# Selective attention and an MLP mixer in one kernel: loads issued behind transposing transfers, and a running sum behind transposes

## The chip, the cores and the metric

The kernel runs on one core of a Trainium2 chip. The time is the device time of one launch in microseconds (us). Several launches are timed and the median is given; one more is profiled.

The engines are called by the profile's names: PE is TensorE (matmuls, and transposes done as matmuls), ACT is ScalarE, DVE is VectorE, POOL is GpSimd, SP is SyncE. Loads of inputs are issued from POOL, outputs and transposing transfers from SP.

## The reference

There are 8 batches of 576 positions, 8 heads of width 64. Attention has an extra bias that comes from the running sum of `s`, and is followed by an MLP mixer over positions and then channels.

```python
scores = scale * np.matmul(q, k.transpose(0, 1, 3, 2))
cum = np.cumsum(np.maximum(s, 0.0), axis=-1)
bias = -(cum[:, :, :, None] - cum[:, :, None, :])
scores = np.where(causal, -1000000000.0, scores + np.minimum(bias, 0.0))
attn = softmax(scores)                  # over the last axis
x = concat_heads(np.matmul(attn, v))    # (8, 576, 512)
xt = x.transpose(0, 2, 1)
h = np.maximum(xt @ w_tok1, 0.0) @ w_tok2
u = x + h.transpose(0, 2, 1)
h2 = np.maximum(u @ w_ch1, 0.0) @ w_ch2
return u + h2
```

## The kernel before, in words

Batches have indices 0 to 7 here. For each of them the kernel records these steps:

- `stage_qk` and `stage_v` issue the loads from POOL: q and k of four heads at a time into a tile `qkn` (a ring of five), v in five parts into `vf` (two). `merge_v` multiplies v by the exponential of the running sum, giving `vp` (one tile for even indices, one for odd). `squares` reads `qkn` on ACT and sums its squares into `sq`, which a test at the end needs; for indices 0 and 1 it has loads of its own, in `stage_sq`.
- `quad` turns q and k of four heads on PE (L689, the 64x64 matmuls). `pair` makes the scores of two heads (L731), exponentials on ACT (L739), a causal mask on DVE (L748), the product with `vp` on PE (L802) and the normalisation on DVE.
- `tok` is the mixer over positions (L899, L961). It leaves u, and u turned, in a tile `uT` (`uTa` for even indices, `uTb` for odd). From index 2 on u is turned by transposing transfers that SP issues (L977), four for an even index and five for an odd one; the fifth reads `us`, the last 64 positions of two batches in one tile.
- `chan` is the mixer over channels: L1017 makes the hidden layer from `uT`, ACT or DVE applies the ReLU, L1042 makes the second layer, DVE adds u (L1050), and SP stores the result (L1055, L1058).

None of this is issued in the order of the record. `Plan.run` is a list scheduler in the kernel's own Python: each step has an engine (or a choice of two), an estimated duration, a priority, and dependencies from the tiles that it reads and writes. The scheduler keeps a clock for each engine and one for the DMA (`dma_free`, first free at 6.0), and adds margins to what waits for a DMA or for PE once its clock passes `STEADY`. The resulting start times give the order of each engine's instructions. On the chip the engines then run in that order and wait on semaphores. Steps with `after` keep a fixed order among themselves: `chain` holds all loads of POOL in the order of their record, and a load waits for the landing of the eighth before it.

The loads are recorded first, all of them: indices 0 and 1 with the weights between, then indices 2 to 7, then the second loads of indices 0 and 1 for their squares. After that come `quad`, `tok` and `chan` of each index. What holds a load back is thus the ring of its tile and the place in `chain`. Where the plan has PE idle in the first 45 us, matmuls on zeros fill it (L1135).

At the start the running sum is made on DVE: `s` is loaded, its ReLU taken (L532), the scan run (L534), half of its last value taken (L537); ACT makes the exponentials `wn` (L540), PE turns them (L560).

Of the kernel before, what the change touches and what calls it, by code (L numbers as in the profile page):

```python
# [8 lines left out]
FP32 = mybir.dt.float32  # L9
# [2 lines left out]
ALU = mybir.AluOpType  # L12


SWITCH = 0.095
STEADY = 50.0
MARGIN = 0.5
# [37 lines left out]
class Plan:  # L55
# [11 lines left out]
    def op(self, alts, reads=(), writes=(), prio=0, dma=0.0, holds=(), after=None, mode=0, lock=False, alone=None):  # L67
        o = Op()
        o.alts = alts
        o.prio = prio  # L70
        o.dma = dma
        o.mode = mode
        o.lock = lock
        o.alone = alone
        o.idx = len(self.ops)
        o.deps = set()
        o.users = []
        o.bufs = []
        for k in list(reads) + list(writes) + list(holds):
            b = k[0] if isinstance(k, tuple) else k  # L80
            if isinstance(b, Buf) and b not in o.bufs:
                o.bufs.append(b)
                b.left += 1
        for k in reads:
            w = self.writer.get(k)
            if w is not None:
                o.deps.add(w)
        for k in writes:
            w = self.writer.get(k)
            if w is not None:  # L90
# [12 lines left out]
        self.ops.append(o)  # L103
        return o

    def run(self, eps=0.03):
# [11 lines left out]
        for o in ops:  # L118
            if o.nd == 0:
                for e in o.alts:  # L120
                    cands[e].append(o)
        dma_free = 6.0
        mode = 0
        order = []

# [17 lines left out]
        while left:  # L143
            best = None
            for e in engines:
                lst = []
                tmin = None
                for o in cands[e]:
                    st = slot_time(o)
# [62 lines left out]
            for u in o.users:  # L212
                if u.after is o:
                    rdy = est + occ
                elif u.alts.keys() == {"PE"} and e == "PE":
                    rdy = est + occ
                elif e in u.alts and len(u.alts) == 1 and not o.dma:
                    rdy = est + occ
                else:
                    rdy = fin  # L220
                    if fin > STEADY:
                        rdy += MARGIN_DMA if o.dma else MARGIN if u.alts.keys() == {"PE"} else 0.0
                u.ready = max(u.ready, rdy)
# [144 lines left out]
def kernel(  # L368
# [18 lines left out]
    NJ = 5  # L387
# [15 lines left out]
    def sb(name, shape, dt, pool=None):  # L403
        return (pool or const).tile(shape, dt, name=name, tag=name)
# [44 lines left out]
    chain = []  # L449
    sent = []  # L450

    def load_op(fn, key, us, occ=0.75, prio=-1):

        o = P.op({"POOL": (occ, 0, fn)}, writes=key, prio=prio, dma=us, after=chain[-1] if chain else None)
        if len(sent) >= 8:
            o.deps.add(sent[-8])
        sent.append(o)
        chain.append(o)

    def load_cast(n, b, h, i, src):  # L460
        def load():
            nc.gpsimd.dma_start(  # L462
                out=n.t[:, i, :, :],
                in_=src[b, h : h + 4, :, :].rearrange("(f e) (p r) d -> (e p) f (r d)", e=2, r=R))
        load_op(load, [(n, i)], 1.45, prio=-1 if b or h else -3)

    qkn = {}

# [47 lines left out]
    for ti, src in enumerate((k, q)):  # L516
# [4 lines left out]
        for f in range(2):  # L521
# [9 lines left out]
         writes=["s"], prio=-7)  # L531
    P.op(dve(576, lambda: nc.vector.tensor_scalar_max(out=s_sb[:, :], in0=s_sb[:, :], scalar1=0.0)),  # L532
         reads=["s"], writes=["sr"], prio=-1)
    P.op({"DVE": (1.3, 1.6, lambda: nc.vector.tensor_tensor_scan(  # L534
        out=cum[:, :], data0=one_sb[:, :], data1=s_sb[:, :], initial=0.0, op0=ALU.mult, op1=ALU.add))},
        reads=["sr"], writes=["cum"], prio=-1)
    P.op(dve(1, lambda: nc.vector.tensor_scalar(  # L537
        out=half[:, :], in0=cum[:, S - 1 : S], scalar1=-0.5, scalar2=None, op0=ALU.mult)),
        reads=["cum"], writes=["half"], prio=-1)
# [59 lines left out]
    def stage_v(b, cs=tuple(range(NJ))):  # L599
        if b not in vbuf:  # L600
            vbuf[b] = Buf(r_vf), Buf(r_vp[b % 2])
        vf, vp = vbuf[b]
        odd = b % 2
        for c in cs:
            n = min(128, S - c * 128)
            p0 = 64 if odd and n < 128 else 0

            def load_first(c=c, n=n, p0=p0):
                nc.sync.dma_start(out=vf.t[p0 : p0 + n, c, :, :],
                                  in_=v[b, :, c * 128 : c * 128 + n, :].rearrange("h p d -> p h d"))  # L610

            def load(c=c, n=n, p0=p0):
                nc.gpsimd.dma_start(out=vf.t[p0 : p0 + n, c, :, :],  # L613
                                  in_=v[b, :, c * 128 : c * 128 + n, :].rearrange("h p d -> p h d"))
            if b == 0 and c == NJ - 1:
                P.op({"SP": (0.6, 5.5, load_first)}, writes=[(vf, c)], prio=-2)
                continue
            load_op(load, [(vf, c)], 1.15 * n / 128, 0.92)
        if b:
            merge_v(b, cs)  # L620

# [50 lines left out]
    def quad(b, h):  # L672
# [4 lines left out]
        for ti in range(2):  # L677
# [6 lines left out]
            def tr(ti=ti, pv=pv):  # L684
                for r in range(R):
                    for e in range(2):
                        p0 = e * PR
                        for f in range(2):
                            nc.tensor.transpose(out=pv(e)[f * D : f * D + D, r * PR : (r + 1) * PR],  # L689
                                                in_=nat.t[p0 : p0 + PR, ti, f, r * D : (r + 1) * D],  # L690
                                                identity=ident[p0 : p0 + PR, p0 : p0 + PR])
            P.op({"PE": (R * 0.031, R * 0.031 + 0.21, tr)}, reads=([(nat, ti, 0), (nat, ti, 1)] if b == 0 and h == 0 else [(nat, ti)]) + ["ident"] + pads,
                 writes=[(pts[e], e) for e in range(2)], holds=[d[ti] for d in dsts], prio=(np_ - 30 * (b < 1 and h < 1), 2), mode=1)
            for e in range(2):
                def ev(eng, ti=ti, e=e, pv=pv):
                    i = pv(e)[:, 0:S].rearrange("d (r p) -> d p r", r=R)
                    o = dsts[e][ti].t[:, 0:S].rearrange("d (p r) -> d p r", r=R)
                    if eng == 0:
                        nc.scalar.copy(out=o, in_=i)  # L699
                    else:  # L700
                        nc.vector.tensor_copy(out=o, in_=i)
                P.op({"ACT": (*c_act(576), lambda ev=ev: ev(0)), "DVE": (*c_dve(576), lambda ev=ev: ev(1))},
                     reads=[(pts[e], e)], writes=[(dsts[e][ti], 0)], prio=1, alone=pts[e])
# [378 lines left out]
    for i in range(2, 4):  # L1082
        load_ch2(i)
    stage_v(1)
    for b in range(2, B):
        stage_qk(b, 0)
        stage_v(b)
        stage_qk(b, 4)
    for b in range(2):
        for h in range(0, H, 4):  # L1090
            stage_sq(b, h)
    for b in range(B):
        for h in range(0, H, 4):
            quad(b, h)
        st = tok(b)
        chan(b, *st)

    P.op({"DVE": (1.3, 1.6, lambda: nc.vector.tensor_tensor_scan(
        out=pre[:, :], data0=one_sb[:, :], data1=wn[:, 0:S], initial=0.0, op0=ALU.mult, op1=ALU.add))},
# [84 lines left out]
```

## Time and profile before

| | before |
|---|---|
| median of three runs | 305.8 us (305.24 to 306.14) |
| the profiled execution | 306.06 us |
| its span, first to last instruction | 304.3 us |
| mean granted PE clock | 0.995 |
| PE busy | 291.8 us (96%) |
| ACT busy | 182.8 us (60%) |
| DVE busy | 172.0 us (57%) |
| POOL busy | 107.6 us (35%) |

Times in the profile count from the first instruction of the span. A row of a timeline gives start, length, engine, line and operation of a run of instructions of one kind, and in brackets the idle time of the engine before it and what ended that. A row of the chain of waits gives start, length, and what the time went to, along the path that ended last. A PE that is called busy is not at its peak, since matmuls are pipelined and their ends are modelled. POOL counts the making of a DMA's descriptors as busy.

### The profile page before, as it was taken

What the parts mean: (1) busy time and instruction counts of PE and PEld (TensorE: products, weight loads), DVE (VectorE), ACT (ScalarE), POOL (GpSimd) and SP (SyncE); (2) the same over time, 40 slices, a digit from 0 to 9 for tenths busy, and PEclk for the clock granted to TensorE, in tenths of its full rate; (3) what the DMA queues carried; (4) which work ended last, traced back from release to release, by engine and by line L of the source; (5) the groups of instructions that cost most, each with busy time, mean ns of one, the idle gap of its engine ahead of it and who ended that gap; (6) DMA issues with size and microseconds to landing.
All of it is one profiled execution on the core that took longest, in us unless ns stands there. A gap on an engine that the chain in (4) does not pass through costs nothing.

```text
span 304.3 us, 8094 instructions
## 1 busy us (share of the span) xinstructions
PE 291.8 (96%) x3430; PEld 168.2 (55%) x3430; DVE 172.0 (57%) x368; ACT 182.8 (60%) x298; POOL 107.6 (35%) x147
## 2 busy tenths in 40 slices
PE   8899999899999999999999999998999999999991
PEld 3478566467754545457754545455764544457550
DVE  5962889377976456756556556956456642420030
ACT  5887884699996486609872387727761286017300
POOL 8675469999780418107620108500000000000000
PEclk9999999999999999999999999999999999999998
DMA  8999999999997673358455535894004310250032
GB/s 218 226 207 206 216 224 229 252 190 262 227 156 125 155 197 54 79 140 178 94 80 103 133 84 83 132 116 136 2 2 84 125 38 0 69 155 2 0 111 74
DMA packets 38348, 39.29 MB, mean 129 GB/s; under 512 B 17600, under 2 KB 30976, under 8 KB 38304
## 3 DMA queue, kind: packets, MB, share of 16 engines
q0 software_dynamic: 17072, 24.25, 44.6%
q1 hardware_dynamic: 21232, 14.44, 18.7%
q8 instruction: 29, 0.48, 0.7%
q14 instruction: 15, 0.12, 0.1%
HBM read 40.65 MB, written 9.44 MB: 165 GB/s over the span
## 4 chain that ended last, share of the span: by engine, by line
PE 84%; DMA 12%; POOL 1%; issue 1%; DVE 0%; POOLq 0%
PE pmx L1017 30%; PE pmx L1042 30%; PE pmx L961 5%; PE pmx L899 5%; PE psc L802 5%; PE psc L731 5%; DMA qkn<-in_k_dram 5%; PE psc L689 3%; DMA wc<-in_moe_w_ch_dram 3%; DMA vf<-in_v_dram 2%; DMA uTb<-us 2%; POOL qkn L462 1%; PE pmx L986 0%; DVE of L1050 0%; POOL keep masks.py:66 0%
## 5 line engine op out<-in xcount | busy, mean ns | idle before, releaser
L1017 PEld LDWEIGHTS <-wc 128*128 128x128 bf16 x624 | 57.9, 98 | 32.6 <-issue 1.5
L739 ACT ACTIVATE E<-psc 128x1024 bf16<-128x1024 f32 x64 | 62.2, 1024 | 22.8 <-PE psc L731 22.2
L1017 PE MATMUL pmx<-uTb,wc 128*128 128x320 bf16 (+2 forms) x384 | 56.1, 299 | 1.4 <-DMA uTb<-ub 1.1
L1042 PE MATMUL pmx<-wc,gb 128*128 128x512 bf16 (+1 forms) x252 | 55.3, 369 | 0.0
L1017 PE MATMUL pmx<-uTa,wc 128*128 128x512 bf16 (+1 forms) x240 | 45.6, 337 | 0.0
L647 ACT ACTIVATE junk<-qkn 128x1152 bf16<-128x1152 bf16 x32 | 37.3, 1166 | 11.7 <-DMA qkn<-in_q_dram 11.3
L1042 PE MATMUL pmx<-wc,ga 128*128 128x512 bf16 x192 | 44.1, 379 | 0.0
L631 POOL TENSOR_TENSOR vp<-vf,wT 128x512 bf16<-128x512 f32 (+1 forms) x31 | 32.3, 1058 | 25.6 <-PE psc L802 24.9
L1024 ACT ACTIVATE gb<-pmx 128x320 bf16<-128x320 f32 (+2 forms) x57 | 24.7, 438 | 21.2 <-PE pmx L1017 17.3
L1042 PEld LDWEIGHTS <-gb 128*128 128x128 bf16 x252 | 23.6, 98 | 24.8 <-issue 0.2
L613 POOL DMA_DIRECT2D vf<-in_v_dram x39 | 34.1, 884 | 7.3 <-DMA qkn<-in_k_dram 2.2
L748 DVE TENSOR_TENSOR E<-E,keep 128x512 bf16<-128x512 bf16 x56 | 25.8, 474 | 13.3 <-ACT E L739 13.1
L1042 PEld LDWEIGHTS <-ga 128*128 128x128 bf16 x192 | 18.2, 98 | 20.4
L1024 ACT ACTIVATE ga<-pmx 128x512 bf16<-128x512 f32 (+1 forms) x36 | 19.2, 535 | 11.7 <-PE pmx L1017 11.1
L462 POOL DMA_DIRECT2D qkn<-in_k_dram x19 | 14.1, 744 | 33.5 <-issue 31.8
L1026 DVE TENSOR_SCALAR gb<-pmx 128x320 bf16<-128x320 f32 (+2 forms) x39 | 18.8, 487 | 11.9 <-PE pmx L1017 11.5
L699 ACT COPY kT<-psc 128x576 bf16<-128x576 bf16 x22 | 13.1, 641 | 19.4 <-PE psc L689 17.9
L802 PEld LDWEIGHTS <-E 128*128 128x128 bf16 x576 | 21.1, 97 | 5.5
L835 DVE TENSOR_TENSOR x<-psc,rc 128x640 bf16<-128x640 f32 x28 | 23.0, 823 | 0.9
L1050 DVE TENSOR_TENSOR of<-pmx,ua 128x512 f32<-128x512 f32 x16 | 11.0, 689 | 19.5 <-PE pmx L1042 19.3
L731 PE MATMUL psc<-qT,kT 64*128 64x256 bf16 (+2 forms) x320 | 21.3, 250 | 0.0
L731 PEld LDWEIGHTS <-kT 64*128 64x128 bf16 x320 | 12.6, 94 | 14.6 <-issue 11.5
(107 smaller groups left out, 300.9 us busy)
## 6 DMA issues: line engine op xcount, KB each, us to landing
vf<-in_v_dram POOLq DMA_DIRECT2D x32, 256.0 KB, 7.9
out_dram<-of SPq DMA_DIRECT2D x31, 256.0 KB, 2.3
qkn<-in_k_dram POOLq DMA_DIRECT2D x19, 288.0 KB, 6.7
qkn<-in_q_dram POOLq DMA_DIRECT2D x19, 288.0 KB, 7.3
wc<-in_moe_w_ch_dram POOLq DMA_DIRECT2D x8, 384.0 KB, 11.4
out_dram<-of SPq DMA_DIRECT2D x10, 128.0 KB, 2.3
vf<-in_v_dram POOLq DMA_DIRECT2D x7, 128.0 KB, 7.4
gb<-in_k_dram SPq DMA_DIRECT2D x1, 576.0 KB, 3.9
```

The lines of the kernel that those rows point to most:

```text
L613: nc.gpsimd.dma_start(out=vf.t[p0 : p0 + n, c, :, :], in_=v[b, :, c * 128 : c * 128 + n, :].rearrange("h p d -> p h d"))
L631: eng.tensor_tensor(out=vp.t[p0 : p0 + n, c, :, 0:D], in0=vf.t[p0 : p0 + n, c, :, :], in1=wT[p0 : p0 + n, cw, b * H : b * H + H].unsqueeze ...
L647: nc.scalar.activation(out=junk[:, :].rearrange("p (t n) -> p t n", t=2), in_=i, func=AF.Square, accum_out=sq[:, col : col + 1])
L731: nc.tensor.matmul(out=ps.t[:, hh * 512 + c0 : hh * 512 + c0 + e - a], lhsT=kT.t[hh * 64 : hh * 64 + 64, j0 : j0 + 128], rhs=qT.t[hh * 64 ...
L739: nc.scalar.activation(out=E.t[:, :, 512 * pc : 512 * pc + 512], in_=ps.t[:, :].rearrange("p (e n) -> p e n", e=2), func=AF.Exp, scale=0.125)
L748: nc.vector.tensor_tensor(out=o, in0=o, in1=keep[:, :].unsqueeze(1).unsqueeze(1).to_broadcast([128, 2, 2, 128]), op=ALU.mult)
L802: nc.tensor.matmul(out=o[:, ic, 0:DE], lhsT=E.t[:, hh, d0 : d0 + 128], rhs=vp.t[:, jc, h + 2 * hh, 0:DE], start=(jc == j_lo), stop=(jc == ic))
L835: nc.vector.tensor_tensor(out=x.t[:, :, :].rearrange("p c (g f e d) -> p g e f c d", f=2, e=2, d=D)[:, h // 4, h % 2], in0=pav2()[:, :, :, ...
L1017: nc.tensor.matmul(out=pm.t[:, 0 : e - a], lhsT=wc1[:, m, cc * 128 : cc * 128 + 128], rhs=uT.t[:, m, a:e], start=(m == 0), stop=(m == NMC ...
L1024: lambda cc=cc, pm=pm, a=a, e=e: nc.scalar.activation(out=g.t[:, cc, a:e], in_=pm.t[:, 0 : e - a], func=AF.Relu),
L1026: lambda cc=cc, pm=pm, a=a, e=e: nc.vector.tensor_scalar_max(out=g.t[:, cc, a:e], in0=pm.t[:, 0 : e - a], scalar1=0.0)),
L1042: nc.tensor.matmul(out=pm.t[:, na:ne], lhsT=g.t[:, cc, c * 128 : c * 128 + 128], rhs=wc2[:, cc, na:ne], start=(cc == 0), stop=(cc == NCC - 1))
```

## The change

- The loads of indices 4 to 7 are no longer recorded with the others at the front. They are recorded after `chan` of indices 2 to 5 (`stage_in(b + 2)`), behind a row of `touch` steps: copies of one element on POOL, each of which reads one chunk of `uT` of index `b` and so waits for the transposing transfer that wrote it. The touches stand in `chain`, and the loads behind them.
- The second loads of indices 0 and 1 are recorded behind the loads of indices 5 and 6.
- The scan of `s` waits, in the plan, for the transposes of q of the first four heads, and its priority among DVE's steps falls from -1 to 2.
- The plan's DMA is first free at 6.85 and not at 6.0. A touch is marked `bare`: the plan adds no margin to what it waits for.
- `probe`, `PACE0`, `PACE1` and `DEPTH` are prepared for touches between loads; with both `PACE` at 0 they issue nothing.

```diff
+DEPTH = 4
+PACE0, PACE1 = 0, 0
 ...
-        dma_free = 6.0
+        dma_free = 6.85
 ...
-                    if fin > STEADY:
+                    if fin > STEADY and not u.bare:
                         rdy += MARGIN_DMA if o.dma else MARGIN if u.alts.keys() == {"PE"} else 0.0
 ...
-    def load_op(fn, key, us, occ=0.75, prio=-1):
+    probes = []
+    seen = sb("seen", [128, 8], FP32, fast)
+
+    def touch(ap, reads, col):
+        o = P.op({"POOL": (0.12, 0.2, lambda: nc.gpsimd.tensor_copy(out=seen[0 : ap().shape[0], col : col + 1], in_=ap()))},
+             reads=reads, writes=[("seen", col)], prio=-1, after=chain[-1])
+        o.bare = True
+        chain.append(o)
+
+    def load_op(fn, key, us, occ=0.75, prio=-1, probe=None):
+        if PACE0 <= len(probes) < PACE1 and probes[-DEPTH]:
+            touch(probes[-DEPTH][0], probes[-DEPTH][1], 0)
+        probes.append((probe, key) if probe else None)
 ...
-    P.op({"DVE": (1.3, 1.6, lambda: nc.vector.tensor_tensor_scan(
+    scan = P.op({"DVE": (1.3, 1.6, lambda: nc.vector.tensor_tensor_scan(
         out=cum[:, :], data0=one_sb[:, :], data1=s_sb[:, :], initial=0.0, op0=ALU.mult, op1=ALU.add))},
-        reads=["sr"], writes=["cum"], prio=-1)
+        reads=["sr"], writes=["cum"], prio=2)
 ...
+            if b == 0 and h == 0 and ti == 1:
+                scan.deps.add(turn)
 ...
-    for b in range(2, B):
+    def stage_in(b):
         stage_qk(b, 0)
         stage_v(b)
         stage_qk(b, 4)
-    for b in range(2):
-        for h in range(0, H, 4):
-            stage_sq(b, h)
+    for b in range(2, 4):
+        stage_in(b)
     for b in range(B):
         for h in range(0, H, 4):
             quad(b, h)
         st = tok(b)
         chan(b, *st)
+        if 2 <= b < B - 2:
+            for c in range(NJ - 1 + b % 2):
+                touch(lambda c=c, uT=st[2]: uT.t[0:1, 0, c * 128 : c * 128 + 1], [(st[2], c)], 1)
+            stage_in(b + 2)
+            if b == 3 or b == 4:
+                for h in range(0, H, 4):
+                    stage_sq(b - 3, h)
```

More of the change, by code (lines that the diff above doesn't have):

```diff
@@ L77, in op @@
         o.users = []
+        o.bare = False
         o.bufs = []
@@ L464, in load @@
                 in_=src[b, h : h + 4, :, :].rearrange("(f e) (p r) d -> (e p) f (r d)", e=2, r=R))
-        load_op(load, [(n, i)], 1.45, prio=-1 if b or h else -3)
+        load_op(load, [(n, i)], 1.45, prio=-1 if b or h else -3, probe=lambda: n.t[0:1, i, 0, 0:1])
     qkn = {}
@@ L617, in stage_v @@
                 continue
-            load_op(load, [(vf, c)], 1.15 * n / 128, 0.92)
+            load_op(load, [(vf, c)], 1.15 * n / 128, 0.92, probe=lambda c=c, p0=p0: vf.t[p0 : p0 + 1, c, 0, 0:1])
         if b:
@@ L691, in tr @@
                                                 identity=ident[p0 : p0 + PR, p0 : p0 + PR])
-            P.op({"PE": (R * 0.031, R * 0.031 + 0.21, tr)}, reads=([(nat, ti, 0), (nat, ti, 1)] if b == 0 and h == 0 else [(nat, ti)]) + ["ident"] + pads,
+            turn = P.op({"PE": (R * 0.031, R * 0.031 + 0.21, tr)}, reads=([(nat, ti, 0), (nat, ti, 1)] if b == 0 and h == 0 else [(nat, ti)]) + ["ident"] + pads,
                  writes=[(pts[e], e) for e in range(2)], holds=[d[ti] for d in dsts], prio=(np_ - 30 * (b < 1 and h < 1), 2), mode=1)
+            if b == 0 and h == 0 and ti == 1:
+                scan.deps.add(turn)
             for e in range(2):
```

## The prediction

> **What bounds the kernel now.** I read the busy time by stretches first, because one share for the whole span hides where TensorE is not the limit. The columns behind each stretch are its length and then the busy time of PE, its weight loads, VectorE (DVE), ScalarE (ACT) and GpSimd (POOL).
>
> ```profile
> 20.00:36.00 16.00, 15.23 (x248) 11.37 (x246) 7.65 (x21) 12.69 (x27) 7.68 (x12) 1.00 1.21 207
> 54.00:60.00 6.00, 4.72 (x47) 2.56 (x46) 1.98 (x4) 3.36 (x5) 5.98 (x7) 1.00 1.05 243
> 60.00:200.00 140.00, 140.00 (x1666) 78.57 (x1663) 92.24 (x184) 97.64 (x152) 64.17 (x80) 1.00 0.70 137
> 200.00:208.00 8.00, 6.61 (x115) 3.53 (x112) 3.76 (x6) 2.50 (x5) 0.00 (x0) 1.00 1.40 175
> 208.00:297.60 89.60, 89.60 (x769) 50.72 (x766) 35.15 (x72) 39.64 (x70) 0.00 (x0) 1.00 0.20 56
> ```
>
> From 60 to 200 and from 208 to 297.6 us PE has no idle time at all, at a granted clock of 1.00. No edit of transfers can shorten those stretches; it can only lengthen them. What can be won lies in the holes: 0.77 us in 20:36, 1.28 in 54:60, 1.39 in 200:208. The timeline of PE names them (start, length, what, and in brackets the idle time before it and who ended it):
>
> ```profile
> 9.22 0.48 PE L689 MATMUL pmx<-ident,qkn 64*64 64x64 bf16 x36 [0.81 <-DMA qkn<-in_k_dram]
> ...
> 35.50 0.48 PE L689 MATMUL psc<-ident,qkn 64*64 64x64 bf16 x36 [0.62 <-DMA qkn<-in_k_dram]
> ...
> 56.08 0.38 PE L899 MATMUL pmx<-x,w 128*128 128x128 bf16 x4 [1.28 <-issue]
> ...
> 206.54 0.70 PE L1017 MATMUL pmx<-uTb,wc 128*128 128x320 bf16 x4 [1.06 <-DMA uTb<-ub]
> 207.57 1.26 PE L1017 MATMUL pmx<-uTb,wc 128*128 128x320 bf16 x8 [0.33 <-DMA uTb<-us]
> ```
>
> Two holes are loads of k that land late at the start, one (56.08) is ended by no engine and no transfer that the profile shows, and the last two, 1.06 + 0.33 = 1.39 us, are PE waiting for the transposing transfers of batch index 5 (the sixth batch).
>
> **The transfers of index 5: minus 1.4 us.** What is normal for them and what happened there is in the view of the tile uTb, first for the stretch 194:208, then for index 7 in 262:272:
>
> ```profile
> DMA to landing us min/median/max: 6.6/8.7/10.5
> ```
>
> ```profile
> DMA to landing us min/median/max: 2.4/2.5/2.5
> ```
>
> The difference is the company. GpSimd's timeline has the last two loads of the kernel (the second look at q and k of index 1, for the squares) issued in the middle of it; the three rows above them are a normal pair of k and q and the five parts of v, which I need below:
>
> ```profile
> 137.21 0.77 POOL L462 DMA_DIRECT2D qkn<-in_k_dram  x1 [14.18 <-issue]
> 137.98 0.72 POOL L462 DMA_DIRECT2D qkn<-in_q_dram  x1
> 138.69 4.25 POOL L613 DMA_DIRECT2D vf<-in_v_dram  x5
> ...
> 193.86 0.77 POOL L462 DMA_DIRECT2D qkn<-in_k_dram  x1 [0.92 <-ACT junk L647]
> 194.62 0.72 POOL L462 DMA_DIRECT2D qkn<-in_q_dram  x1
> ```
>
> After the change these second looks are issued with the loads of indices 5 and 6, behind the transfers of indices 3 and 4, and the loads of index 7 wait until the transfers of index 5 have landed. Nothing of GpSimd's queue is then in flight beside index 5, so its transfers should land in about 2.5 us and the 1.39 us go. Next in line on PE is the channel matmul itself, in order, with no other wait before it. I take all of it: -1.4 (bounds 0 if something else slows them, and -1.4; PE cannot give back more than it idles).
>
> **The start: minus 0.6 and minus 0.4.** Two edits act here. The planner's first free moment of the DMA moves from 6.0 to 6.85, so it expects each load later, and the running sum of s waits for the transposes of q. In the built order PE then places the scores of the first pair ahead of the transposes that idled 0.81 us at 9.22, and two more groups of channel matmuls of index 0 ahead of the transposes that idled 0.62 us at 35.50. The loads themselves stand in GpSimd's queue as before, so that load still lands at 35.5, but PE has less left to do by then. The hole at 35.50 is worth -0.6 (bounds -0.6 and 0). Of the hole at 9.22 I take half, -0.4: the first exponential comes earlier, but the weights exp(sum of s), and with them the scaled v, come later, and which of the two ends last I cannot read (bounds -0.8 and +0.4, the second as much lost as I expect won).
>
> **What the change adds.** Eighteen one-element copies on GpSimd (four or five for each of indices 2 to 5), each waiting for one transposing transfer. They are no longer than a DMA issue there, 0.77 us, so at most 14 us on an engine that is idle for 75.8 of the 140 us quoted above. What counts is what stands behind them in GpSimd's order: q, k and v of the batch two ahead, and the products of v (vp). The tight case is index 5, behind the transfers of index 3. SyncE's timeline gives when those are issued, and the tile views of qkn and vf in 137:143 give the landing of loads:
>
> ```profile
> 126.95 6.03 SPq L977 DMA_TRANSPOSE uTb<-ub  x4
> 133.08 1.21 SPq L977 DMA_TRANSPOSE uTb<-us  x1
> ...
> 262.96 5.12 SPq L977 DMA_TRANSPOSE uTb<-ub  x4
> 268.18 1.22 SPq L977 DMA_TRANSPOSE uTb<-us  x1
> ```
>
> ```profile
> DMA to landing us min/median/max: 5.4/6.1/6.8
> ```
>
> ```profile
> DMA to landing us min/median/max: 7.3/7.8/8.6
> ```
>
> On the old clock, the last transfer of index 3 lands at 133.08 + 2.4 = 135.5. Then k is issued, q at 136.3, landed by 136.3 + 6.8 = 143.1; the last part of v is out 0.77 + 0.72 + 4.25 = 5.7 us after the first and lands 7.8 later, at 149.0. Who needs them is in the chain of waits (start, length, what):
>
> ```profile
> 142.07 0.55 PE psc L731 x10
> 142.62 1.19 PE pmx L1017 x8
> 143.81 0.54 PE psc L802 x18
> ...
> 150.33 0.73 PE psc L689 x72
> ...
> 156.15 0.86 PE pmx L1042 x4
> 157.01 0.54 PE psc L802 x18
> ...
> 170.41 0.73 PE psc L689 x72
> 171.14 0.97 PE pmx L1042 x4
> ```
>
> PE turns k and q of index 5 at 150.33, 7.2 us after they landed, and multiplies by its v at 157.01, 8.0 us after the last part landed, which leaves room for the product of that part. So PE does not wait for these loads directly: 0 (if both covers were gone, each microsecond of lateness would be one on PE).
>
> ScalarE is the weak point. In its built order the square of the newly loaded q and k of index 5 stands right in front of the exponentials of the last head pair of index 4, whose scores are the L731 at 142.07. The page has the square's price and its habit of waiting:
>
> ```profile
> L647 ACT ACTIVATE junk<-qkn 128x1152 bf16<-128x1152 bf16 x32 | 37.3, 1166 | 11.7 <-DMA qkn<-in_q_dram 11.3
> ```
>
> With q at 143.1 the square ends at 144.3, so the exponentials, due at 142.07 + 0.55 = 142.6, are 1.7 us late, and the L802 at 143.81, which needs a score tile that they free, with them. That is the upper bound, 1.7 for each of indices 5 and 7, 3.4 in all. The lower bound is 0: undisturbed, the fifth transfer follows the first by 268.18 - 262.96 = 5.2 and not by 133.08 - 126.95 = 6.1 us, and with a landing of 5.4 the square ends at 142.0, in time. Squares have already waited 11.3 us for loads in the old profile (the last entry of this row), while the holes of PE quoted above come to 4.1 us in all and have other releasers. I take 0.35 each, +0.7, nearer to the lower bound for that row.
>
> Last, PE's order has 60 visits to the 64-row matmuls (transposes and scores) where it had 56. The chain shows what a return costs: four L1042 take 0.86 us, and 0.97 straight behind a visit. Four visits more are 4 x 0.11 = +0.4 (bounds 0, where the visit stood beside a wait anyway, and +0.8, if the way in costs as much).
>
> **A rule against the change.** The Trainium skill, page "DMA: Bandwidth & Descriptors", section "Rules for kernel authors", says to issue a DMA early, compute, and wait on it late, since its fixed cost is then hidden; holding loads back goes against that. By it alone the first bound above (+3.4) would be the likely one. In this trace the early loads are those that the transfers of index 5 collided with (landing 6.6 to 10.5 us against 2.5).
>
> **The sum.** -1.4 - 0.6 - 0.4 + 0.7 + 0.4 = -1.3 us. The profiled execution took 306.06 us (span 304.3 and 1.76 around it, which stay), so 304.8 for a profiled one like it; against the median of 305.8 it is 304.5. I hold 0.3%, 0.9 us, for about what a measurement of this kernel can tell from no change: faster below 304.9, slower above 306.7.
>
> **Rivals.**
> - *The squares hold up ScalarE* (slower). The mechanism above at its upper bound: 3.4 in place of 0.7 makes -1.3 + 2.7 = +1.4, so 307.2. For it: the landing of 6.8 and the order on ScalarE. Against: the 11.3 us of such waits that cost PE little. It becomes slower by over 0.9 us once each of the two places costs more than (0.9 + 2.0) / 2 = 1.45 us, which is q landing 6.5 us or more after its issue with the fifth transfer as late as at 133.08.
> - *The gain of the start is lost again* (no change to speak of). The hole at 56.08 falls inside a group of matmuls and has no releaser, so PE probably lacked instructions there while the DMA was full (share 1.05 in 54:60). If that is tied to the DMA's progress and not to PE's, PE that arrives 1.0 us earlier waits 1.0 longer: -0.3, so 305.5.
> - *That hole goes* (faster still). Five more filler matmuls shift where the instruction stream breaks; if the supply then arrives in time, -1.3 - 1.3 = -2.6, so 303.2.
> - *The transfers are slow for another reason* (the change doesn't do what it says). Then the 1.4 stay: +0.1, so 305.9. Against it: index 7, with no load in flight, has 2.5 us.
>
> **How the numbers follow.** Forecast 0.50, squares 0.17, start lost 0.12, hole gone 0.14, transfers slow 0.07. The forecast lies 0.4 us inside the bound of faster; with its terms' bounds I count 0.43 of its 0.50 as faster, 0.05 as same and 0.02 as slower. Hole gone adds 0.14 and a corner of the start rival 0.02 to faster, 0.59. Same is 0.05 + 0.10 + 0.05 from the last rival = 0.20. Slower is 0.02 + 0.17 + 0.02 = 0.21. The range reaches from the hole gone with a little more at the start, 302.9, to the squares at nearly their full price, 306.9.
>
> **What would show it.** In the profile of the changed kernel the transfers of index 5 should land in about 2.5 us and PE should be busy without a hole from 200 to 208. The hole at 35.50 should be under 0.1 us. ScalarE should wait for loads of q four times or more, at the squares of indices 5 and 7, with at most some tenths of PE idle beside each. The products of v of indices 4 to 7 should end before PE's L802 asks for them. The prediction is wrong if PE shows waits on ScalarE of over 1 us there, if the products end last, or if the transfers still take over 5 us with no load in flight.

## The result and the profile after

The changed kernel takes 318.0 us (median of six runs, 316.6 to 320.0) against 304.9 us beside it: 1.043 times as long, 95% interval 1.038 to 1.048. The prediction was 304.5 us, faster. The profiled execution took 319.6 us, its span is 317.9 us against 304.3 before. Here and below, a ratio and its interval leave out executions more than 1.5% above the fastest of the same kernel, and a median takes them all.

The same stretches as before, from the busy time by stretches (PE, its weight loads, DVE, ACT, POOL, granted clock, DMA share, GB/s; the last stretch is longer here):

```profile
20.00:36.00 16.00, 15.65 (x254) 12.32 (x253) 7.06 (x23) 13.08 (x32) 8.40 (x14) 1.00 1.20 207
54.00:60.00 6.00, 5.95 (x91) 3.56 (x91) 2.73 (x7) 4.48 (x8) 5.98 (x8) 1.00 0.93 214
60.00:200.00 140.00, 129.84 (x1545) 73.56 (x1559) 93.07 (x169) 82.54 (x131) 55.73 (x80) 0.98 0.59 122
200.00:208.00 8.00, 7.84 (x60) 3.88 (x59) 4.89 (x11) 7.58 (x12) 0.00 (x0) 1.00 0.09 27
208.00:311.00 103.00, 100.84 (x904) 56.39 (x912) 44.69 (x89) 45.14 (x77) 13.37 (x19) 1.00 0.35 84
```

What was to be won seems to be there: the holes at 35 and 56 are gone, and the tile uTb in 204:216 shows the transfers of index 5 landing as quickly as those of index 7 did, where they took 6.6 to 10.5 us before:

```profile
DMA to landing us min/median/max: 2.4/2.4/2.7
```

But from 60 to 200 us, where PE had no idle time at all, it now idles 140.00 - 129.84 = 10.2 us. Its timeline names the larger holes and who ended each:

```profile
67.15 0.38 PE L1003 MATMUL pmx<-ident,us 128*128 128x128 bf16 x4 [3.30 <-DVE of L1067]
...
124.30 0.40 PE L748 MATMUL psc<-qT,kT 64*128 64x256 bf16 x4 [0.83 <-ACT qT L716]
...
150.78 0.70 PE L819 MATMUL psc<-vp,E 128*128 128x65 bf16 x18 [0.55 <-ACT E L756]
...
154.36 0.27 PE L819 MATMUL psc<-vp,E 128*128 128x65 bf16 x3 [1.13 <-DVE E L765]
156.11 0.51 PE L819 MATMUL psc<-vp,E 128*128 128x65 bf16 x11 [1.48 <-DVE E L773]
...
196.81 0.61 PE L819 MATMUL psc<-vp,E 128*128 128x65 bf16 x14 [0.89 <-DVE E L765]
...
227.19 0.70 PE L819 MATMUL psc<-vp,E 128*128 128x65 bf16 x18 [1.43 <-ACT E L756]
```

None is ended by a load or by GpSimd. There are two families. The larger is ended by VectorE, by its masks of E (L765, L773), or by work queued behind them (at 67.15). VectorE's timeline at the first of these holes, and then GpSimd's for the same time, each with the same place of the kernel before ahead of it:

```profile
62.49 0.76 DVE L748 TENSOR_TENSOR E<-E,keep 128x512 bf16<-128x512 bf16 x2
```

```profile
61.90 3.42 DVE L765 TENSOR_TENSOR E<-E,keep 128x512 bf16<-128x512 bf16 x2
65.25 1.13 DVE L773 TENSOR_TENSOR E<-E,keep 128x128 bf16<-128x128 bf16 x1
66.41 0.69 DVE L1067 TENSOR_TENSOR of<-pmx,ua 128x512 f32<-128x512 f32 x1
```

```profile
61.78 0.73 POOL L462 DMA_DIRECT2D qkn<-in_k_dram  x1
62.47 0.74 POOL L462 DMA_DIRECT2D qkn<-in_q_dram  x1
63.20 1.09 POOL L631 TENSOR_TENSOR vp<-vf,wT 128x512 bf16<-128x512 f32 x1
64.24 4.28 POOL L613 DMA_DIRECT2D vf<-in_v_dram  x5
```

```profile
62.96 5.43 POOL L646 TENSOR_TENSOR vp<-vf,wT 128x512 bf16<-128x512 f32 x5
```

Two masks take 3.42 us instead of 0.76, while GpSimd runs five products of v back to back. Before, the issues of index 4's loads stood between these products. Of the 56 long masks (128x512) after, the 48 that overlap no product have a median of 0.417 us; the slow ones (up to 3.02 us) all overlap products. Before, six overlapped products, and the slowest took 1.26 us. The Trainium skill, page "SBUF — State Buffer", section "Who interferes with whom", says that a VectorE instruction with two inputs in SBUF contends with a GpSimd instruction that reads SBUF, since its second input comes through a read interface that the two share. This trace agrees. The groups by line give the sum (busy, mean ns, idle before), VectorE's mask before (L748), then after (L765):

```profile
L748 DVE TENSOR_TENSOR E<-E,keep 128x512 bf16<-128x512 bf16 x56 | 25.8, 474 | 13.3 <-ACT E L739 13.1
```

```profile
L765 DVE TENSOR_TENSOR E<-E,keep 128x512 bf16<-128x512 bf16 x56 | 31.6, 569 | 18.5 <-ACT E L756 18.3
```

The second family is ended by ScalarE. Its timeline before the hole at 227.19 shows a square that waits 2.10 us for the late q of index 7, with the exponentials behind it:

```profile
224.97 1.16 ACT L662 ACTIVATE junk<-qkn 128x1152 bf16<-128x1152 bf16 x1 [2.10 <-DMA qkn<-in_q_dram]
...
226.13 1.92 ACT L756 ACTIVATE E<-psc 128x1024 bf16<-128x1024 f32 x2
```

And there is a third cost, which no hole shows. One-microsecond stretches behind the 3.30 us of idle time (the third number from the end is the granted clock):

```profile
68.00:69.00 1.00, 1.00 (x5) 0.47 (x4) 0.24 (x1) 1.00 (x3) 0.39 (x1) 0.72 0.64 236
69.00:70.00 1.00, 1.00 (x8) 0.45 (x7) 0.00 (x0) 1.00 (x2) 0.00 (x0) 0.50 0.05 14
70.00:71.00 1.00, 1.00 (x18) 0.86 (x16) 0.05 (x1) 0.97 (x3) 0.00 (x0) 0.50 0.00 0
71.00:72.00 1.00, 1.00 (x4) 0.29 (x2) 0.97 (x2) 0.68 (x2) 0.00 (x0) 0.57 0.00 0
```

PE counts as busy, but at half clock: 0.28 + 0.50 + 0.50 + 0.43 = 1.7 us lost. The same happens from 157 to 161 us, behind the holes of 1.13 and 1.48. So 10.2 us of idle time, 3.4 of half clock and the 1.43 at 227 make 15.0; less the holes of before that are gone (0.62, 1.28 and 1.39), 11.7 of the 13.6 us by which the span grew. The busy times of the two pages close the sum: PE idles 317.9 - 296.0 = 21.9 us against 304.3 - 291.8 = 12.5, 9.4 more, and counts as busy 4.2 us longer, of which the half clock is 3.4. So the 1.9 us that remain are 1.1 of small gaps and 0.8 of busy time.

### The profile page after: what moved, and what is told of

Same layout as the page of the kernel before. It is cut to its first block, busy times and chain, and to the rows that moved or that the text cites. A ratio compares the mean times of both kernels' runs of the same rounds, so it can differ in the third digit from the quotient of the medians.

```text
span 317.9 us, 8073 instructions
## 1 busy us (share of the span) xinstructions
PE 296.0 (93%) x3400; PEld 170.3 (54%) x3435; DVE 184.4 (58%) x375; ACT 178.4 (56%) x291; POOL 111.4 (35%) x165
## 4 chain that ended last, share of the span: by engine, by line
PE 69%; DMA 11%; DVE 8%; ACT 5%; POOL 3%; issue 2%; SPq 0%; ACTq 0%; POOLq 0%; DVEq 0%
PE pmx L1059 23%; PE pmx L1034 22%; DMA qkn<-in_q_dram 7%; PE pmx L916 5%; PE psc L748 4%; PE pmx L978 4%; PE psc L819 3%; DVE E L765 3%; PE psc L704 2%; PE pmx L1158 2%; ACT E L756 2%; ACT junk L662 2%; DMA uTb<-us 2%; DMA uTb<-ub 2%; POOL vf L628 1%
## 5 line engine op out<-in xcount | busy, mean ns | idle before, releaser
L1034 PE MATMUL pmx<-uTb,wc 128*128 128x320 bf16 (+2 forms) x384 | 57.6, 306 | 0.0
L1059 PE MATMUL pmx<-wc,gb 128*128 128x512 bf16 (+1 forms) x243 | 54.4, 369 | 0.7 <-issue 0.3
L1034 PE MATMUL pmx<-uTa,wc 128*128 128x512 bf16 (+1 forms) x233 | 44.4, 336 | 0.7 <-issue 0.5
L662 ACT ACTIVATE junk<-qkn 128x1152 bf16<-128x1152 bf16 x32 | 37.3, 1165 | 11.1 <-DMA qkn<-in_q_dram 10.8
L765 DVE TENSOR_TENSOR E<-E,keep 128x512 bf16<-128x512 bf16 x56 | 31.6, 569 | 18.5 <-ACT E L756 18.3
L1041 ACT ACTIVATE gb<-pmx 128x320 bf16<-128x320 f32 (+2 forms) x54 | 23.3, 435 | 22.9 <-PE pmx L1034 19.5
L628 POOL DMA_DIRECT2D vf<-in_v_dram x39 | 33.4, 870 | 6.0 <-DMA wc<-in_moe_w_ch_dram 3.3
L819 PEld LDWEIGHTS <-E 128*128 128x128 bf16 x576 | 21.7, 98 | 12.2 <-issue 2.9
L1043 DVE TENSOR_SCALAR gb<-pmx 128x320 bf16<-128x320 f32 (+2 forms) x42 | 20.6, 491 | 10.7 <-PE pmx L1034 10.2
L819 PE MATMUL psc<-vp,E 128*128 128x65 bf16 x522 | 21.4, 195 | 5.5 <-DVE E L765 2.0
L716 ACT COPY kT<-psc 128x576 bf16<-128x576 bf16 x24 | 14.4, 640 | 21.3 <-PE psc L704 17.5
L748 PE MATMUL psc<-qT,kT 64*128 64x256 bf16 (+2 forms) x320 | 21.9, 251 | 1.9 <-ACT qT L716 0.8
L1043 DVE TENSOR_SCALAR ga<-pmx 128x512 bf16<-128x512 f32 (+1 forms) x27 | 15.3, 572 | 11.6 <-PE pmx L1034 11.4
L748 PEld LDWEIGHTS <-kT 64*128 64x128 bf16 x320 | 12.7, 94 | 16.8 <-issue 14.9
```

Source lines behind the costliest of these rows:

```text
L628: nc.gpsimd.dma_start(out=vf.t[p0 : p0 + n, c, :, :], in_=v[b, :, c * 128 : c * 128 + n, :].rearrange("h p d -> p h d"))
L662: nc.scalar.activation(out=junk[:, :].rearrange("p (t n) -> p t n", t=2), in_=i, func=AF.Square, accum_out=sq[:, col : col + 1])
L748: nc.tensor.matmul(out=ps.t[:, hh * 512 + c0 : hh * 512 + c0 + e - a], lhsT=kT.t[hh * 64 : hh * 64 + 64, j0 : j0 + 128], rhs=qT.t[hh * 64 ...
L765: nc.vector.tensor_tensor(out=o, in0=o, in1=keep[:, :].unsqueeze(1).unsqueeze(1).to_broadcast([128, 2, 2, 128]), op=ALU.mult)
L819: nc.tensor.matmul(out=o[:, ic, 0:DE], lhsT=E.t[:, hh, d0 : d0 + 128], rhs=vp.t[:, jc, h + 2 * hh, 0:DE], start=(jc == j_lo), stop=(jc == ic))
L1034: nc.tensor.matmul(out=pm.t[:, 0 : e - a], lhsT=wc1[:, m, cc * 128 : cc * 128 + 128], rhs=uT.t[:, m, a:e], start=(m == 0), stop=(m == NMC ...
```

## The experiments

Theory P: GpSimd's products of v now run in rows beside VectorE's masks. Theory S, the rival in the prediction: the squares wait for late loads in front of ScalarE's exponentials and copies. The first four kernels ran together, kernel before at 305.4 us.

**Products cut short**

```
+                w_ = D if b < 3 else 1
 ...
-                    out=vp.t[p0 : p0 + n, c, :, 0:D], in0=vf.t[p0 : p0 + n, c, :, :],
+                    out=vp.t[p0 : p0 + n, c, :, 0:w_], in0=vf.t[p0 : p0 + n, c, :, 0:w_],
 ...
```

> The changed kernel with the products of v of indices 3 to 7 computed for one column in 64 (the rest of the scaled v is left as an earlier index wrote it); the order on every engine is that of the changed kernel. Theory P (GpSimd's products hold off VectorE's masks): the idle stretches of PE at 67.15 (3.30 us), 154.36 and 156.11 (1.13 and 1.48) and 196.81 (0.89) go, 6.8 us in all, and with them the stretches at a granted clock of about 0.5 that follow the two largest (68 to 72 and 157 to 161 us, some 3.7 us lost); 318.0 - 10.5 = 307.5 us, with no mask (L765) over 0.7 us. Theory S (the squares hold up ScalarE): these masks are late for another reason, the time stays within 1 us of 318.

Measured: 312.3 us (ratio 1.023, 1.019 to 1.027), 5.7 less than the changed kernel and not the 10.5 expected. Every hole ended by a mask is gone, and no long mask takes over 0.47 us. The timeline of PE shows what is left, ended by ScalarE (there are also 0.49 ended by ScalarE and 0.40 ended by VectorE's copy of qT):

```profile
119.98 0.40 PE L749 MATMUL psc<-qT,kT 64*128 64x256 bf16 x4 [1.47 <-ACT qT L717]
...
156.12 1.01 PE L749 MATMUL psc<-qT,kT 64*128 64x256 bf16 x10 [1.75 <-ACT kT L717]
...
220.67 0.70 PE L820 MATMUL psc<-vp,E 128*128 128x65 bf16 x18 [1.53 <-ACT E L757]
```

So P is real, but half of what it was expected to be. ScalarE's wait for q grew from 10.8 to 13.1 us, and half clock came here too, behind the 1.75 us.

**Squares freed from the loads**

```
+    def sqsrc():
+        return wc1[:, 0, 0 : 2 * R * D].rearrange("p (t n) -> p t n", t=2)
 ...
-            P.op({"ACT": (1.25, 1.6, lambda e=e, col=col: square(col, n.t[:, :, e, :]))},
+            P.op({"ACT": (1.25, 1.6, lambda e=e, col=col: square(col, n.t[:, :, e, :] if 1 < b < 4 else sqsrc()))},
 ...
```

> The changed kernel with the squares of indices 0, 1 and 4 to 7 taken of weights that are long in place instead of the loaded q and k, so that ScalarE waits for no load there (the sums that they check are then not those of q and k). The order on every engine is that of the changed kernel. Theory S (squares hold up ScalarE, the rival of the prediction): most of the loss goes, 318.0 to about 306. Theory P (products hold off masks): only the idle stretches of PE that ScalarE ends go, 0.83 + 0.40 at 124, 0.55 at 150.78 and 1.43 at 227.19, 3.2 us, so about 314.8, and the stretch of 3.3 us at 67 with its half clock stays as it is.

Measured: 308.2 us, 9.8 less. But its four executions form two pairs, 305.0 and 305.8, and 310.7 and 311.9; the faster pair is 0.999 times the kernel before (0.995 to 1.003). In either pair S is larger than theory P had it. The profiled execution is the one of 310.7. It has the collision at 62 us and one more, both of family P:

```profile
66.92 0.59 PE L1006 MATMUL pmx<-ident,us 128*128 128x128 bf16 x4 [3.86 <-DVE of L1070]
...
189.01 0.95 PE L822 MATMUL psc<-vp,E 128*128 128x65 bf16 x18 [0.70 <-DVE E L768]
```

Half clock lasts until 2.74 us after the first hole, which makes 1.4 us more: 3.86 + 1.4 = 5.2, about as much as lies between the pairs. So the faster pair probably ran without this collision, but no profile of it was kept.

**The start alone** (the two edits of the start, with the loads issued as before)

> The kernel before with the edits of the start alone (sum of s behind the transposes of q, the planner's DMA free from 6.85); all loads are issued as before. If the late loads carry the whole loss: faster by 0.6 to 1.0 us as predicted for the start (304.0 against 304.9), with the stretch of 0.62 us at 35.50 gone and the transfers of index 5 still at 6.6 to 10.5 us. If the start's new order carries part of it: over 306, with a row of back-to-back products of v beside VectorE's masks at 60 to 70 us.

Measured: 304.5 us, ratio 0.9963 (0.9934 to 0.9991). The start carries no loss. One thing came out otherwise than expected: the transfers of index 5 land in 3.2 to 6.1 us where they took 6.6 to 10.5, although the last two loads are still issued beside them (at 194.96 and 195.72), and PE no longer waits for them. So the company of these two loads is not the whole reason for the slow transfers; what else differs, no run shows. Busy time by stretches:

```profile
200.00:208.00 8.00, 7.95 (x125) 4.48 (x124) 4.71 (x8) 2.82 (x7) 0.00 (x0) 1.00 0.99 198
```

**A gate on the last two loads alone** (on the kernel before)

```
+    for b, h in ((0, 0), (0, 4), (1, 0)):
+        stage_sq(b, h)
 ...
+        if b == 5:
+            touch(lambda uT=st[2]: uT.t[0:1, 0, 512:513], [(st[2], 4)], 1)
+            stage_sq(1, 4)
```

> The kernel before with one edit: the last two loads (the second look at q and k of index 1, heads 4 to 7) stand behind a one-element copy that waits for the last transposing transfer of index 5. Nothing of GpSimd's other work is moved. If these two loads alone slow the transfers of index 5: the transfers land in about 2.5 us, the 1.06 + 0.33 us of idle PE at 206 go, 304.9 - 1.4 = 303.5. If the transfers are slow for another reason, 304.9 and the idle stretches stay.

Measured: 305.8 us, ratio 0.9997 (0.9968 to 1.0026): nothing. The transfers do land in 2.5 to 4.6 us and PE does not wait for them. But the timeline of PE has two holes that the profile of before did not have:

```profile
64.69 0.38 PE L1001 MATMUL pmx<-ident,us 128*128 128x128 bf16 x4 [1.14 <-DVE of L1065]
...
214.01 0.70 PE L817 MATMUL psc<-vp,E 128*128 128x65 bf16 x18 [0.79 <-ACT E L754]
```

The second follows from the edit: ScalarE's square of the late loads waits 1.46 us for q there, with exponentials behind it. The first does not: in the 8 us ahead of it GpSimd's and VectorE's rows stand in the order of the kernel before, and one mask took 1.10 us beside a product. So the place at 60 to 66 us can be hit in one execution and missed in another.

**Both cures together** (short products and freed squares, so work is left out; the kernel before at 305.6 us in this group)

> The changed kernel with both: products of v of indices 3 to 7 cut to one column in 64, and the squares of indices 0, 1 and 4 to 7 taken of weights in place. Apart, the two took 5.7 us (products) and about 10 us (squares) off the 318.0. If products and squares are the whole loss and both hit the same masks: 302 to 304 us, under the kernel before, with the gain of the start (0.9) and of the transfers of index 5 (1.4) at last seen. If the late loads cost something of their own (PE waiting for k, q or v): over 305, with idle stretches of PE ended by DMA or by the transposes.

Measured: 303.4 us, ratio 0.9939 (0.9911 to 0.9968). PE by stretches, with the late loads and all their copies still in place:

```profile
60.00:200.00 140.00, 140.00 (x1665) 78.44 (x1663) 91.12 (x185) 90.81 (x142) 38.01 (x81) 1.00 0.62 126
200.00:208.00 8.00, 8.00 (x125) 4.92 (x124) 4.65 (x10) 4.56 (x8) 6.23 (x10) 1.00 0.85 169
```

Medians in us, and for the kernel with two pairs the middle of each:

| | squares wait for loads | squares freed |
|---|---|---|
| products whole | 318.0 | 308.2 (305.4 and 311.3) |
| products short | 312.3 | 303.4 |

With the products short, the squares cost 312.3 - 303.4 = 8.9 us; with the products whole, 318.0 - 305.4 = 12.6 or, with the collision, 318.0 - 311.3 = 6.7. The products cost 5.7 us while the squares wait, and 2.0 or 7.9 once these are freed. Together the two are 14.6 us, the whole loss. How it is divided between them is not settled, since the collision at 62 us comes and goes. Nothing else of the late loads had to be paid for in these runs.

**Late order without the waits** (the eighteen copies left out)

> The changed kernel without the eighteen one-element copies: the loads of indices 4 to 7 are recorded as late as in the changed kernel, but wait for no transposing transfer. If the wait makes the loss (loads land late, the squares wait for them): the squares' waits for q fall from 10.8 us to under 4 and the time to 306 to 309, with the row of five products beside the masks at 62 to 68 us left as it is. If the recorded order alone makes it: 315 or more.

Measured: 309.5 us (ten executions, 307.0 to 315.2), ratio 1.0105 (1.007 to 1.0139). ScalarE's wait for q falls to 4.4 us. The row of five products is gone too, against the expectation: without the copies, index 4's loads are issued between the products again. So this run takes away much of P along with S. The new hole is at the transfers of index 3, with which the loads now collide (they land in 5.2 to 11.3 us); it is followed by half clock from 140.0 to 143.4:

```profile
140.07 2.29 PE L1034 MATMUL pmx<-uTb,wc 128*128 128x320 bf16 x8 [2.48 <-DMA uTb<-ub]
```

**Squares behind the transposes of the same loads** (the changed kernel, nothing left out)

```
+            if b > 3 and ti == 1:
+                for o in behind.get((b, h), ()):
+                    o.deps.add(turn)
 ...
```

Here `behind` holds the squares of the same loads.

> The changed kernel with each square of indices 4 to 7 placed behind the transposes of the same loads (the second looks of indices 0 and 1 behind the first transposes of indices 6 and 7): a square can then no longer wait for a load in front of exponentials. Nothing is left out. Theory S: as good as squares that read weights in place, about 307, without idle stretches of PE ended by ScalarE's qT, kT or E at 124, 151 and 227. If the squares cost by their place on ScalarE and not by waiting: no gain, 318. The row of products at 62 to 68 us and its 3.3 us stay in either case.

Measured: 308.9 us, ratio 1.0109 (1.007 to 1.0149). This real edit is worth 9.1 us, as much as the freed squares, so they cost by waiting (4.0 us for q instead of 10.8) and not by their own time (37.4 us, 37.3 before). What is left in PE's timeline of the profiled execution (306.7 us) is family P:

```profile
64.29 0.38 PE L1008 MATMUL pmx<-ident,us 128*128 128x128 bf16 x4 [1.48 <-DVE of L1072]
...
116.31 0.48 PE L824 MATMUL psc<-vp,E 128*128 128x65 bf16 x10 [0.69 <-DVE E L778]
...
148.75 0.51 PE L824 MATMUL psc<-vp,E 128*128 128x65 bf16 x11 [0.59 <-DVE E L778]
```

**Start, gate on the last two loads, and their squares late**

> The kernel before with the edits of the start, the gate on the last two loads alone (behind the last transposing transfer of index 5), and the squares of those two loads behind the last exponentials of index 7, where nothing is left for them to hold up. The start gave 0.9 and the gate alone nothing, since 0.79 of its 1.39 us came back as a wait for the exponentials at 214. If that wait was the moved square: 304.5 - 1.4 = 303.1 (ratio 0.992). If it has another cause: 304.5.

Measured: 304.8 us, ratio 0.9952 (0.9927 to 0.9977), no better than the start alone: there, the wait that the gate removes was gone already. It and the start alone beat the kernel before, by 0.4 to 0.5%.

**The loads alone** (the changed kernel without the edits of the start)

> The changed kernel without the edits of the start: only the loads are moved. The start alone gave 0.9 us, so if the parts add up: 318.0 + 0.9 = about 319 (ratio 1.044), with the row of products at 62 to 68 us and the squares' waits as in the changed kernel. If the start's order makes the collisions at 62 to 68 us: under 314, without the 3.3 us before the transposes there.

Measured: 318.1 us (316.2 to 323.1), ratio 1.0393 (1.0345 to 1.0441), within the spread of the changed kernel. The loads carry the loss; whether the start's 0.9 us is still in the changed kernel, these runs cannot tell.

**Index 4 as before, squares behind**

> The changed kernel with the squares behind the transposes of the same loads, and with the loads of index 4 issued as in the kernel before (the copies gate indices 5 to 7 alone). If the moved issues of index 4's loads were what held GpSimd's products of index 3 apart: from 60 to 70 us no row of five products, no idle PE before L1008's successor (1.48 us with the squares behind alone, 3.3 in the changed kernel), 308.9 - 1.5 to 3 = 306 to 307.4. If the row comes from another edit: it stays, 308.9.

Measured: 310.2 us, ratio 1.0147 (1.0104 to 1.0189): no gain, against the expectation. The hole at 64 us shrank to 0.56 us, but the timeline of PE has a larger one at a mask of index 4's last pair:

```profile
151.34 0.79 PE L824 MATMUL psc<-vp,E 128*128 128x65 bf16 x11 [4.12 <-DVE E L778]
```

VectorE's timeline has that mask, the short one, which takes 0.22 us elsewhere. GpSimd's shows what runs beside it, the products of index 5's late v:

```profile
146.81 4.47 DVE L778 TENSOR_TENSOR E<-E,keep 128x128 bf16<-128x128 bf16 x1
```

```profile
147.36 1.05 POOL L647 TENSOR_TENSOR vp<-vf,wT 128x512 bf16<-128x512 f32 x1
148.35 0.76 POOL L477 DMA_DIRECT2D qkn<-in_q_dram  x1
149.14 3.17 POOL L647 TENSOR_TENSOR vp<-vf,wT 128x512 bf16<-128x512 f32 x3
```

**Products on VectorE, squares behind**

> The changed kernel with the squares behind the transposes, and the products of v of indices 3 to 7 on VectorE instead of GpSimd; nothing is left out, all loads and their copies as in the changed kernel. If the masks are late because GpSimd's products run at the same time, every mask of the second half takes under 0.6 us, and the time falls to about 304 to 305.5 (308.9 less the idle 1.48, 0.69 and 0.59 and a half clock behind the first), though VectorE gets some 25 x 0.65 = 16 us more work. If VectorE has no room for it: 309 or more, with PE idle on VectorE.

Measured: 314.6 us, ratio 1.0304 (1.0263 to 1.0345): slower, against the expectation. The masks are quick again (mean 0.436 us), so it was GpSimd's products that held them. But now the products wait for v in VectorE's own queue, as its groups show, and PE behind them (1.3 to 2.2 us, four times in the profiled execution, which took 310.3 us):

```profile
L647 DVE TENSOR_TENSOR vp<-vf,wT 128x512 bf16<-128x512 f32 (+1 forms) x34 | 22.8, 683 | 12.1 <-DMA vf<-in_v_dram 11.9
```

**Products on VectorE, loads as before** (with the edits of the start)

> The kernel before with the edits of the start, and the products of v of indices 3 to 7 on VectorE; loads as before. The start alone is 304.5 with PE busy nearly throughout from 60 us on (its holes there come to under 1.5 us), so there is little to win: 303.5 to 304.5 if VectorE has room for 16 us more, 306 or more if not.

Measured: 305.7 us, ratio 1.0016 (0.9991 to 1.004). No mask is held up (mean 0.418 us) and nothing waits for v (0.2 us), yet nothing is won: with early loads, the products on GpSimd cost no more than their 16 us on VectorE do.

**Spacers** (the changed kernel, with fills where issues had stood)

```
+    for i in range(11):
+        P.op({"POOL": (0.52, 0.6, lambda: nc.gpsimd.memset(zero[:, :], 0.0))}, writes=["zero2"], prio=-1, after=chain[-1])
+        chain.append(P.ops[-1])
```

> The changed kernel, and eleven fills of a small constant tile on GpSimd (an estimate from one fill of 64x528 that took 0.53 us there: 5.7 us in all, as long as the seven issues of index 4's loads that stood there before) between the last load of index 3 and the products of index 3. Nothing else is moved. If the moved issues had kept the products of index 3 off VectorE's masks: the masks at 62 to 66 us take their 0.4 us again, the 3.30 us of idle PE at 67 and the half clock behind it (some 1.7 us) go, 318.0 - 5 = 313. If the row of products collides wherever it stands, or does not matter: the stretch stays or comes 6 us later, 318.

Measured: 313.6 us, ratio 1.0258 (1.0224 to 1.0291): 4.5 less than the changed kernel, as expected. GpSimd's timeline, and VectorE's masks:

```profile
62.44 6.39 POOL L1109 MEMSET zero<- 128x512 bf16 x11
68.80 5.16 POOL L646 TENSOR_TENSOR vp<-vf,wT 128x512 bf16<-128x512 f32 x5
```

```profile
61.62 0.76 DVE L765 TENSOR_TENSOR E<-E,keep 128x512 bf16<-128x512 bf16 x2
```

Eleven fills that do nothing make the changed kernel 1.4% faster. The seven issues of index 4's loads had kept GpSimd's products out of the masks' way, and moving them let GpSimd run ahead.

**v early, q and k late, squares behind**

> The changed kernel with the squares behind the transposes, and the loads of v issued ahead of the copies, as early as the two buffers of v allow; only q and k stand behind the transposing transfers. With the squares behind alone it took 308.9. If what was left is the lateness of v (its products run late and in a row beside the masks): 304 to 306. If early v only moves the rows of products to other masks, or slows the transfers again: 308 or more.

Measured: 312.4 us, ratio 1.0199 (1.0124 to 1.0274). The masks are nearly quick (mean 0.442 us). Late v was thus the rest of P, or the issues of v, which again stand between the products here (two from 61.98 us, three from 64.75 us), space them; this run does not tell which. But the loads of v now run beside the transfers of index 5, which land in 9.7 to 13.2 us, and PE waits as it never did before the change:

```profile
211.61 4.98 PE L1039 MATMUL pmx<-uTb,wc 128*128 128x320 bf16 x20 [6.12 <-DMA uTb<-ub]
```

## Why the prediction was wrong, step by step

- **The transfers of index 5, -1.4.** The step was right that they land quickly behind gated loads and that PE then has no hole at 206. It was wrong that the two loads are the whole reason: in the start alone they are still issued beside the transfers, these land in 3.2 to 6.1 us, and PE does not wait. No run shows the 1.4 as time won: the gate alone gives nothing, and the gate with the start no more than the start.
- **The start, -1.0.** The size came out, 0.9 us, but by luck. PE begins the mixer of index 0 at 20.1 to 20.9 us in the three profiles without the start's edits and at 19.8 to 21.7 in the thirteen with them, so the hole at 9.22 won nothing; in the changed kernel matmuls on zeros stand there. From that mixer to the first scores after 55 us PE takes 36.3 to 37.0 us without these edits and 35.0 to 35.9 with them. The hole at 35.50 explains little of it: the gate alone and the loads alone have none there either. What shrinks is the hole at 56, from 0.85 to 1.28 us without to at most 0.82 with them. That was the rival "that hole goes", which had 0.14; whether its reason was right, no run shows.
- **The squares, +0.7 (bounds 0 and 3.4).** The right mechanism, the rival's, with the wrong size: 8.9 us with the products short, above the upper bound. The step looked at indices 5 and 7 and at 1.7 us each. With the products short, ScalarE ends 1.47 us of idle time at index 4 (and 0.40 follow there, ended by VectorE's copy of qT), 1.75 at 5, 0.49 at 6 and 1.53 at 7, and half clock behind the 1.75 adds 1.7: 7.3 us. The second pair of loads of index 4, whose squares stand in front of copies of qT (the hole at 124), was not weighed at all. The 11.3 us of such waits in the old profile, which spoke for the lower bound, fell where PE had other work; after the change 10.8 us fell in front of exponentials and copies. The sum of a wait said nothing of its cost. One sign that the prediction had named came: PE waits 1.43 us on ScalarE at 227.19.
- **The products of v, left out.** The step on "what the change adds" asked only whether PE waits for them, and there it was right: no hole is ended by GpSimd. It did not ask who else is held while they run. The loads that were moved past them had been their spacers, as the fills show. This is the step that failed in kind, 5.7 us in the changed kernel.
- **Direct waits for loads, 0.** True for PE, but the slack of 8.0 us for v was not slack for its products: put on VectorE, they wait 11.9 us for v.
- **An idle microsecond priced at one.** Twice in the changed kernel, 1.7 us of half clock came on top.
- **The two gains together.** With short products and freed squares the kernel is 305.6 - 303.4 = 2.2 us faster than before, where these steps had 2.4. That kernel leaves out work that the kernel before does, so the 2.2 do not confirm them.
- **Four more visits to the 64-row matmuls, +0.4.** Not told apart by any run.

## What to carry to other kernels

Before moving a load, list what its issue instruction separates on its own queue, and what its neighbours there share with other engines: here seven idle-looking issues kept two engines out of each other's way. A wait that costs nothing where it stands can cost its full length, and more, once work that PE needs is queued behind it, so price every instruction behind a moved load, not only its direct reader. When a loss has two suspects, take each away alone and then both: the square of four times says more than any single trace. Look at the single executions too, since here one of the four cells was two groups, some 6 us apart.

## What the runs showed of the hardware

Idle stretches of PE cost more than their length when they fall in the wrong place. In the sixteen profiles the granted clock fell to 0.50 ten times while the kernel worked, seven times for 3.413 us and three times for 6.827 (the loads alone, index 4 as before, and v early). Within a profile the clock changes only on a grid of 3.413 us, and the grid starts elsewhere in each profile. Cut by this grid, every one of the ten full-clock stretches ahead of half clock has PE busy for less than half of its length (0 to 0.48), and none of the other 1359 is under 0.55. Rows of two profiles show it, of short products and then of the spacers (length and PE's busy time come first, the granted clock is third from the end):

```profile
153.43:156.84 3.41, 1.51 (x15) 0.92 (x15) 1.40 (x4) 3.41 (x7) 0.00 (x0) 1.00 1.13 193
```

```profile
143.07:146.48 3.41, 1.97 (x20) 1.24 (x15) 1.69 (x4) 0.92 (x1) 1.33 (x3) 1.00 1.07 251
146.48:149.90 3.42, 2.13 (x30) 1.71 (x30) 2.15 (x2) 3.42 (x7) 3.29 (x5) 1.00 1.17 182
149.90:153.31 3.41, 1.34 (x23) 0.95 (x22) 3.38 (x4) 0.86 (x3) 3.39 (x4) 1.00 1.21 206
```

The hole of 1.75 us in short products lies in one stretch, and half clock follows. The hole of 2.74 us with the spacers (145.03 to 147.77) is cut in two by the grid, and the clock stays; the holes of 1.35 and 0.72 us behind it share the next stretch, and half clock follows from 153.3. A stretch at half clock in which PE has work throughout costs 1.7 us. The Trainium skill, page "TensorE: Matmul & The Clock Gate", section "Part 1: The HAM clock gate (the "warmup" mystery)", describes a free-running window of about 3.4 us, after an idle one of which the clock is halved. The length and the free grid agree with these profiles, but the window need not be idle: one busy for 0.48 sufficed. The same page's section "HAM oscillation — how this bites in real kernels" speaks of idle gaps over about 3.4 us, and here, where the two differ, a gap of 1.75 us sufficed.

A row of products can hold one VectorE instruction for longer than one product takes (some 1.05 us): a single mask took up to 3.02 us in the changed kernel, and the short one 4.47 us with index 4 as before, where it ended only some 1.0 us ahead of the row.
